# Sliding-window attention with a low-rank mixer: later loads of the low-rank factors, a last tile in halves, and one batch transposed by DMA

## Chip, cores and metric

The kernel runs on one core of a Trainium2 chip. The metric is the device time of one execution in microseconds (us), smaller is better.

## The reference

```python
def _attn_ref(q, k, v):                       # q, k, v: [8, 8, 576, 64]
    scores = (1.0 / np.sqrt(64)) * np.matmul(q, k.transpose(0, 1, 3, 2))
    rel = pos[:, None] - pos[None, :]
    scores = np.where((rel >= 0) & (rel < 64), scores, -1e9)
    attn = softmax(scores)                    # (shortened here)
    return np.matmul(attn, v)

def _moe_ref(x, U, V, w_ch1, w_ch2):          # x: [8, 576, 512], U: [576, 32], V: [32, 576]
    h = x.transpose(0, 2, 1) @ U @ V          # mixes the 576 positions, rank 32
    u = x + h.transpose(0, 2, 1)
    ch = np.maximum(u @ w_ch1, 0.0) @ w_ch2   # MLP, 512 -> 2048 -> 512
    return u + ch
```

The attention output, with the heads side by side, is the `x` of the mixer. Inputs and output are float32. The kernel computes in bf16.

## The kernel before

The output has 8 x 576 = 4608 tokens, and the MLP goes over them in nine chunks of 512. A chunk is a row of "slots": 16 of the first MLP matmul (four TensorE matmuls each, tile `psA`), then 16 quarters of the second (tile `psU`). The attention and the mixer of the next batch are spread over these slots by tables such as `PLACE_2`, so that TensorE does them between MLP matmuls. Batch 0 has no chunk to hide in: everything it needs is the startup, and the first MLP matmul cannot start before it.

The low-rank factors are loaded first of all by SyncE, and the loads that GpSimd issues run beside them:

```python
    load_v(0)                                     # GpSimd; k and q of batch 0 were issued before
    # ... some memsets on VectorE, two of them on uf
    nc.sync.dma_start(
        out=uf[0][:, 0:NFULL, :], in_=moe_U[0 : NFULL * P, :].rearrange("(c p) r -> p c r", p=P)
    )                                             # 512 rows of 128 B
    nc.sync.dma_start(out=uf[0][0:W, NFULL, :], in_=moe_U[NFULL * P : S, :])
    nc.sync.dma_start(out=uf[1][W:P, 0, :], in_=moe_U[0:W, :])
    nc.sync.dma_start(
        out=uf[1][:, 1:NT, :], in_=moe_U[W:S, :].rearrange("(c p) r -> p c r", p=P)
    )
    for g in range(4):
        nc.sync.dma_start(out=vf[g * R : (g + 1) * R, :], in_=moe_V[:, :])   # 32 rows of 2304 B
    w1v = moe_w_ch1.rearrange("(c p) n -> p c n", p=P)
    for lo, hi in ((0, 1024), (1024, 2048)):
        nc.gpsimd.dma_start(out=w1b[:, :, lo:hi], in_=w1v[:, :, lo:hi])      # cast to bf16 on the way
    # ... k, q and v of batch 1, then w2b
```

The startup's main row, and what uses the factors (`K` and `Q` are transposes of k and q by TensorE with the copies behind them, `S` the scores, `PV` the attention output, `U` the product with U, `HT` the product with V):

```python
    for what in ("K0", "K1", "Q0", "Q1", "S0", "S1", "K2", "K3", "Q2", "Q3", "S2", "S3"):
        # ... emits that piece
        turn_over({"K1": 3, "Q1": 1, "S0": 1, "K3": 1, "Q3": 1}.get(what, 0))   # idle matmuls
    # ...
    for i in range(2):
        nc.scalar.copy(out=ub[i][:], in_=uf[i][:])                # ScalarE: U to bf16
    nc.scalar.copy(out=vrep[:, W : W + S], in_=vf[:])             # ScalarE: V to bf16
    for t in range(NT + 2):
        # ... PV(t), XT(t - 2), U(t - 2)
    for f in [a["U"][NT - 1]] + a["X3"] + a["HT"]:
        f()                 # U's last piece copies hh on ScalarE; HT needs hh and vrep
```

From batch 2 on, k and q are transposed by the DMA crossbar, on SyncE's queue; u (the input of the MLP, which must have its features on the partitions) is transposed by TensorE in batches 0 to 2 and by the crossbar from batch 3 on:

```python
    NXU = 3
        def TX(t):                                # k and q of a batch >= 2
            def f():
                for dst, src in ((kx, kb), (qx, qb)):
                    nc.sync.dma_start_transpose(out=dst[:, t, :, :], in_=...)
            return f

        def UT(t):
            def f():
                # ...
                if b >= NXU:
                    nc.sync.dma_start_transpose(out=dst, in_=u_tiles[g][:])
                    return
                tp = ps_tp.tile([P, NDC, P], BF16, name="tpu", tag="tp")
                for dc in range(NDC):
                    nc.tensor.transpose(tp[:, dc, :], u_tiles[g][:, dc * P : (dc + 1) * P], ident[:])
                nc.scalar.copy(out=dst, in_=tp[:])
            return f

    PLACE_2 = {                                   # slots of chunk 1, which carries batch 2
        # ...
        "UTP": [5],                               # batch 1's last transpose
        "TX": [12, 13, 14, 15, 16],               # k and q of batch 3
        "U": [19],
        "V": [21, 22, 23],                        # up-projection: u = V part + x
        "UT": [23, 24, 25, 26, 27],               # u of batch 2
    }
```

SyncE also issues the stores of the outputs (`ch2`, one store of 256 KB per 128 tokens). A store is in program order with the transposes on SyncE.

The softmax here doesn't subtract the row's maximum and nothing guards it: scores larger than these inputs give would overflow.

## Time and profile before

| | us |
|---|---|
| median of the first three runs | 329.75 |
| median of the four runs compared with the kernel after | 330.23 |
| span of the profiled run, granted clock 0.998 | 328.3 |
| first MLP matmul of chunks 0, 1, 2, 3 starts | 24.95, 64.77, 101.54, 135.21 |
| last TensorE instruction starts | 324.19 |

The profile's times count from the start of the span. "L560" is source line 560; the lines of the changed kernel are numbered a little higher, for it is longer. PE is TensorE, DVE VectorE, ACT ScalarE, POOL GpSimd, and SPq is SyncE's sequencer, which issues DMAs. `out<-in` names the tiles.

Here are lines of the page of the kernel before: engine busy time, then the busy tenths in 40 slices of the span (a digit of 9 is 90% or more) for TensorE, its granted clock and the DMA engines, then the chain of waits that ended last.

```profile
span 328.3 us, 6734 instructions
...
PE 316.2 (96%) x2802; PEld 147.9 (45%) x2802; DVE 172.2 (52%) x308; ACT 94.7 (29%) x143; POOL 102.9 (31%) x134
...
PE   6889999989999999999999999999999999999995
...
PEclk9999999999999999999999999999999999999999
DMA  8999999999999999999996993354300330021011
...
## 4 chain that ended last, share of the span: by engine, by line
PE 86%; DVE 5%; ACT 3%; DMA 3%; issue 2%; POOL 1%; POOLq 0%
PE psU L582 38%; PE psA L560 34%; PE xr L364 4%; DMA qg<-in_q_dram 3%; PE sc L311 3%; ACT pts L329 3%; PE psv L486 2%; DVE pts L331 1%; PE pshh L396 1%; DVE un L499 1%; PE tpg L258 1%; PE psht L396 0%; PE psh L396 0%; PE tpu L518 0%; PE ua 
...
```

TensorE is busy for 96% of the span and holds 86% of the chain, at full clock. The DMA engines are nearly full over the first half. What moves the time is therefore when TensorE starts its MLP, and where it waits afterwards.

The startup first. The timeline of ScalarE before shows the casts of U, U and V and the copies of hh (start and duration in us, engine, line, operation; in brackets the idle time before it and what ended it):

```profile
16.97 0.34 ACT L675 CAST ub_97<-uf_95 128x160 bf16<-128x160 f32 x1
17.18 0.35 ACT L675 CAST ub_98<-uf_96 128x160 bf16<-128x160 f32 x1
17.41 0.69 ACT L676 CAST vrep<-vf 128x576 bf16<-128x576 f32 x1
...
23.05 0.65 ACT L406 CAST hh<-psh 128x256 bf16<-128x256 f32 x2 [4.95 <-PE psh L396]
```

And the timeline of TensorE before, first HT matmuls and first MLP matmuls:

```profile
23.47 0.60 PE L464 MATMUL uam<-vrep,hh 128*128 128x512 bf16 x2
...
24.95 1.02 PE L560 MATMUL psA<-uTc,w1b 128*128 128x512 bf16 x4 [0.44 <-DVE uTc L473]
```

The casts are done by 18.1 us, 5 us before ScalarE needs to copy hh. hh ends the startup: the last V load landed at 12.50 us and had slack. The loads of U landed at 2.77, 6.76, 8.22 and 10.76 us.

SyncE next. The timeline of SyncE before: the first issue and the V issues at the start, then the last transpose of batch 3 in chunk 1 and the store behind it. For a transpose the second column is its time on the sequencer.

```profile
0.81 0.45 SPq L199 DMA_DIRECT2D uf_95<-in_moe_U_dram  x1
...
3.97 2.24 SPq L208 DMA_DIRECT2D vf<-in_moe_V_dram  x4
...
92.12 2.54 SPq L280 DMA_TRANSPOSE qf<-qn_111  x1
94.75 8.04 SPq L594 DMA_DIRECT2D out_dram<-osb  x4
```

From 77.43 to 94.66 us SyncE does nothing but batch 3's ten transposes. A store that was ready at 89.5 us leaves at 94.75 and lands at 101.55.

In the waits of TensorE over chunk 1 before (engine, tile, line, waited for: total us, times, longest) there is one only:

```profile
PE tpu L518 <- DVE un L499: 1.1, 1, 1.1
```

### The profile page before, as it was taken

What the parts mean: (1) busy time and instruction counts of PE and PEld (TensorE: products, weight loads), DVE (VectorE), ACT (ScalarE), POOL (GpSimd) and SP (SyncE); (2) the same over time, 40 slices, a digit from 0 to 9 for tenths busy, and PEclk for the clock granted to TensorE, in tenths of its full rate; (3) what the DMA queues carried; (4) which work ended last, traced back from release to release, by engine and by line L of the source; (5) the groups of instructions that cost most, each with busy time, mean ns of one, the idle gap of its engine ahead of it and who ended that gap; (6) DMA issues with size and microseconds to landing.
All of it is one profiled execution on the core that took longest, in us unless ns stands there. A gap on an engine that the chain in (4) does not pass through costs nothing.

```text
span 328.3 us, 6734 instructions
## 1 busy us (share of the span) xinstructions
PE 316.2 (96%) x2802; PEld 147.9 (45%) x2802; DVE 172.2 (52%) x308; ACT 94.7 (29%) x143; POOL 102.9 (31%) x134
## 2 busy tenths in 40 slices
PE   6889999989999999999999999999999999999995
PEld 2444544434454444444444444444444444444442
DVE  4564682378645844584548553765376425115211
ACT  3435641028223530344025401540063001301400
POOL 8591878536536855417700500000000000000000
PEclk9999999999999999999999999999999999999999
DMA  8999999999999999999996993354300330021011
GB/s 114 179 208 195 170 189 169 148 155 175 131 134 208 165 137 154 207 174 141 145 209 98 134 140 112 62 86 103 105 4 2 73 106 32 2 82 45 0 66 64
DMA packets 151871, 39.56 MB, mean 121 GB/s; under 512 B 140960, under 2 KB 146080, under 8 KB 151840
## 3 DMA queue, kind: packets, MB, share of 16 engines
q0 software_dynamic: 100096, 18.36, 78.9%
q1 hardware_dynamic: 51744, 20.77, 35.5%
q8 instruction: 22, 0.36, 0.5%
q14 instruction: 9, 0.07, 0.1%
HBM read 37.14 MB, written 9.44 MB: 142 GB/s over the span
## 4 chain that ended last, share of the span: by engine, by line
PE 86%; DVE 5%; ACT 3%; DMA 3%; issue 2%; POOL 1%; POOLq 0%
PE psU L582 38%; PE psA L560 34%; PE xr L364 4%; DMA qg<-in_q_dram 3%; PE sc L311 3%; ACT pts L329 3%; PE psv L486 2%; DVE pts L331 1%; PE pshh L396 1%; DVE un L499 1%; PE tpg L258 1%; PE psht L396 0%; PE psh L396 0%; PE tpu L518 0%; PE ua L447 0%
## 5 line engine op out<-in xcount | busy, mean ns | idle before, releaser
L560 PE MATMUL psA<-uTc,w1b 128*128 128x512 bf16 x576 | 133.7, 380 | 2.3 <-DVE uTc L473 0.4
L560 PEld LDWEIGHTS <-w1b 128*128 128x128 bf16 x576 | 53.3, 98 | 63.3 <-issue 2.9
L591 DVE TENSOR_TENSOR osb<-psU,un 128x512 f32<-128x512 f32 x36 | 24.8, 689 | 78.0 <-PE psU L582 78.0
L329 ACT ACTIVATE pts<-sc 128x1024 bf16<-128x1024 f32 x32 | 31.3, 1023 | 8.8 <-PE sc L311 7.3
L331 DVE TENSOR_TENSOR pts<-pts,maskA 128x1024 bf16<-128x1024 bf16 x28 | 19.3, 691 | 10.2 <-ACT pts L329 10.2
L135 POOL DMA_DIRECT2D vA_105<-in_v_dram x16 | 14.1, 885 | 29.4 <-DVE c_9_2735 L569 18.3
L499 DVE TENSOR_TENSOR un<-psv,xs_102 128x512 bf16<-128x512 f32 (+1 forms) x20 | 13.0, 683 | 10.4 <-PE psv L486 10.4
L135 POOL DMA_DIRECT2D vA_104<-in_v_dram x16 | 14.1, 887 | 13.4 <-PE xr L364 7.9
L499 DVE TENSOR_TENSOR un<-psv,xs_103 128x512 bf16<-128x512 f32 (+1 forms) x20 | 13.0, 684 | 8.6 <-PE psv L486 8.4
L364 PEld LDWEIGHTS <-pts 128*64 128x64 bf16 x512 | 11.2, 110 | 10.4 <-issue 4.1
L126 POOL DMA_DIRECT2D kn_108<-in_k_dram x15 | 12.7, 847 | 10.1 <-DMA vA_105<-in_v_dram 5.8
L126 POOL DMA_DIRECT2D qn_110<-in_q_dram x15 | 12.7, 848 | 8.7 <-DMA qn_110<-in_q_dram 4.5
L126 POOL DMA_DIRECT2D kn_109<-in_k_dram x15 | 12.8, 857 | 6.4 <-DMA vA_104<-in_v_dram 3.9
L373 DVE RECIPROCAL rcp<-xr 128x8 f32<-128x8 f32 (+1 forms) x40 | 8.2, 204 | 12.8 <-PE xr L364 12.4
L311 PEld LDWEIGHTS <-kf 64*64 64x64 bf16 x704 | 10.1, 107 | 10.2 <-issue 9.1
L374 DVE TENSOR_TENSOR xs_103<-xr,rcp 128x512 bf16<-128x512 f32 (+1 forms) x20 | 13.8, 692 | 0.7
L374 DVE TENSOR_TENSOR xs_102<-xr,rcp 128x512 bf16<-128x512 f32 (+1 forms) x20 | 13.8, 690 | 0.7
L126 POOL DMA_DIRECT2D qn_111<-in_q_dram x15 | 12.8, 855 | 2.8 <-DMA qn_111<-in_q_dram 2.1
L486 PE MATMUL psv<-hh,vrep 128*128 128x512 bf16 x40 | 12.6, 379 | 0.0
L311 PE MATMUL sc<-qf,kf 64*64 64x128 bf16 (+1 forms) x576 | 11.2, 214 | 0.0
L635 PE MATMUL unread<-idle 128*128 128x512 bf16 x16 | 6.4, 524 | 1.3 <-DVE idle L156 1.3
L364 PE MATMUL xr<-vA_105,pts 128*64 128x65 bf16 x160 | 7.2, 197 | 0.2 <-DVE xs_103 L374 0.2
(553 smaller groups left out, 510.0 us busy)
## 6 DMA issues: line engine op xcount, KB each, us to landing
out_dram<-osb SPq DMA_DIRECT2D x36, 256.0 KB, 3.0
vA_104<-in_v_dram POOLq DMA_DIRECT2D x16, 128.0 KB, 8.1
w1b<-in_moe_w_ch_dram POOLq DMA_DIRECT2D x2, 1024.0 KB, 15.0
vA_105<-in_v_dram POOLq DMA_DIRECT2D x16, 128.0 KB, 11.5
w2b<-in_moe_w_ch_dram POOLq DMA_DIRECT2D x4, 512.0 KB, 12.6
kn_108<-in_k_dram POOLq DMA_DIRECT2D x12, 128.0 KB, 11.9
qn_110<-in_q_dram POOLq DMA_DIRECT2D x12, 128.0 KB, 13.2
kn_109<-in_k_dram POOLq DMA_DIRECT2D x12, 128.0 KB, 10.8
```

Source lines behind the costliest of these rows:

```text
L126: nc.gpsimd.dma_start(out=dst[0:rows, t, :, :], in_=src[b, :, t * P : t * P + rows, :].rearrange("h p d -> p h d"),)
L135: nc.gpsimd.dma_start(out=va[:, t, :, 0:D], in_=v[b, :, t * P : (t + 1) * P, :].rearrange("h p d -> p h d"),)
L311: nc.tensor.matmul(sc[r0 : r0 + W, g, col * W : (col + n) * W], keys_of(j, u, rs), queries_of(j, blk, n, rs), start=not spare, stop=last o ...
L329: nc.scalar.activation(out=dst, in_=sc[:], func=ACT.Exp, scale=scale)
L331: nc.vector.tensor_tensor(out=dst, in0=dst, in1=maskA.rearrange("p g n w -> p g (n w)"), op=ALU.mult)
L364: nc.tensor.matmul(xr[r0 : r0 + W, h // 4, (h % 4) * VW : (h % 4 + 1) * VW], pts[:, h // 2, h % 2, blk, :] if blk < NB - 1 else ptl[:, h / ...
L374: nc.vector.tensor_tensor(out=x[lo:hi, t, :, :].rearrange("p (a h) d -> p a h d", a=2), in0=xv[:, :, :, 0:D], in1=rcp[lo:hi].to_broadcast( ...
L486: nc.tensor.matmul(ps[0][:, n, :], vrep[:, off : off + P], hh["sb"][:], start=True, stop=True)
L499: nc.vector.tensor_tensor(out=u_tiles[g][rs, :], in0=ps[0][rs, n, :], in1=x[rs, t, :, :].rearrange("p h d -> p (h d)"), op=ALU.add,)
L560: nc.tensor.matmul(ps[:], w1b[:, dc, i * P : (i + 1) * P], uTc[:, :, dc, :], start=(dc == 0), stop=(dc == NDC - 1),)
L582: nc.tensor.matmul(acc[t][:], c1[i][:, t * P : (t + 1) * P], w2b[:, i, :], start=(i == 0), stop=(i == NFC - 1),)
L591: nc.vector.tensor_tensor(out=osb[:], in0=acc[t][:], in1=u_tiles[g][:], op=ALU.add)
```

## The change

It has three parts. (1) The loads of U and V leave only after the copy of K3 (small memsets on VectorE into their tiles make SyncE wait for VectorE), so that q, k and v of batch 0 get the DMA engines first. (2) The last output tile of 128 tokens is computed in two halves of 256 columns, and each half is stored by two queues, to shorten the end. (3) u of batch 2 is transposed by the crossbar in place of TensorE, its up-projection comes one slot sooner, the transposes follow in slots 20 to 22, and batch 1's last transpose moves from slot 5 to 7.

```diff
-    NXU = 3
+    NXU = 2
...
-    nc.vector.memset(uf[0][:, NT - 1, :], 0.0)
-    nc.vector.memset(uf[1][:, 0, :], 0.0)
...
-    (the eight nc.sync.dma_start of U and V, as above)
+    def load_low_rank():
+        for part in (uf[0][:, NT - 1, :], uf[0][:, 0, 0:1], uf[1][:, 0, :], uf[1][:, 1, 0:1], vf[:, 0:1]):
+            nc.vector.memset(part, 0.0)
+        (the same eight nc.sync.dma_start)
...
+        def ch2_last(t, quarter):
+            def f():
+                ...
+                half = quarter // 2
+                cs = slice(half * DM // 2, (half + 1) * DM // 2)
+                ...                       # 8 matmuls per quarter, 256 columns each
+                if quarter % 2 == 1:
+                    osb = out_pool.tile([P, DM], FP32, name="osb")[:, 0 : DM // 2]
+                    nc.vector.tensor_tensor(out=osb, in0=acc[half][:], in1=u_tiles[g][:, cs], op=ALU.add)
+                    for r0, queue in ((0, nc.sync), (W, nc.scalar)):
+                        queue.dma_start(
+                            out=outf[g * P + r0 : g * P + r0 + W, cs], in_=osb[r0 : r0 + W, :]
+                        )
+            return f
+
         def ch2(t, quarter):
+            if c == NCH - 1 and t == TPC - 1:
+                return ch2_last(t, quarter)
...
     PLACE_2 = {
-        "UTP": [5],
+        "UTP": [7],
...
-        "V": [21, 22, 23],
-        "UT": [23, 24, 25, 26, 27],
+        "V": [20, 21, 22],
+        "UT": [20, 21, 21, 22, 22],
     }
...
             a["T"][2 * j + (what[0] == "Q")]()
+        if what == "K3":
+            load_low_rank()
```

More of the change, by code (lines that the diff above doesn't have):

```diff
@@ L196 @@
         nc.vector.memset(qn[i][W:P, NFULL, :, :], 0.0)
-    nc.sync.dma_start(
-        out=uf[0][:, 0:NFULL, :], in_=moe_U[0 : NFULL * P, :].rearrange("(c p) r -> p c r", p=P)
-    )
-    nc.sync.dma_start(out=uf[0][0:W, NFULL, :], in_=moe_U[NFULL * P : S, :])
-    nc.sync.dma_start(out=uf[1][W:P, 0, :], in_=moe_U[0:W, :])
-    nc.sync.dma_start(
-        out=uf[1][:, 1:NT, :], in_=moe_U[W:S, :].rearrange("(c p) r -> p c r", p=P)
-    )
-    for g in range(4):
-        nc.sync.dma_start(out=vf[g * R : (g + 1) * R, :], in_=moe_V[:, :])
+    def load_low_rank():
+        for part in (uf[0][:, NT - 1, :], uf[0][:, 0, 0:1], uf[1][:, 0, :], uf[1][:, 1, 0:1], vf[:, 0:1]):
+            nc.vector.memset(part, 0.0)
+        nc.sync.dma_start(
+            out=uf[0][:, 0:NFULL, :], in_=moe_U[0 : NFULL * P, :].rearrange("(c p) r -> p c r", p=P)
+        )
+        nc.sync.dma_start(out=uf[0][0:W, NFULL, :], in_=moe_U[NFULL * P : S, :])
+        nc.sync.dma_start(out=uf[1][W:P, 0, :], in_=moe_U[0:W, :])
+        nc.sync.dma_start(
+            out=uf[1][:, 1:NT, :], in_=moe_U[W:S, :].rearrange("(c p) r -> p c r", p=P)
+        )
+        for g in range(4):
+            nc.sync.dma_start(out=vf[g * R : (g + 1) * R, :], in_=moe_V[:, :])
     w1v = moe_w_ch1.rearrange("(c p) n -> p c n", p=P)
@@ L574, in mlp @@
         acc = {}
+        def ch2_last(t, quarter):
+            def f():
+                g = c * TPC + t
+                half = quarter // 2
+                cs = slice(half * DM // 2, (half + 1) * DM // 2)
+                if quarter % 2 == 0:
+                    acc[half] = psum["mm"].tile([P, DM // 2], FP32, name="psL", tag="mm")
+                for i in range(8 * (quarter % 2), 8 * (quarter % 2) + 8):
+                    nc.tensor.matmul(
+                        acc[half][:],
+                        c1[i][:, t * P : (t + 1) * P],
+                        w2b[:, i, cs],
+                        start=(i == 0),
+                        stop=(i == NFC - 1),
+                    )
+                if quarter % 2 == 1:
+                    osb = out_pool.tile([P, DM], FP32, name="osb")[:, 0 : DM // 2]
+                    nc.vector.tensor_tensor(
+                        out=osb, in0=acc[half][:], in1=u_tiles[g][:, cs], op=ALU.add
+                    )
+                    for r0, queue in ((0, nc.sync), (W, nc.scalar)):
+                        queue.dma_start(
+                            out=outf[g * P + r0 : g * P + r0 + W, cs], in_=osb[r0 : r0 + W, :]
+                        )
+            return f
         def ch2(t, quarter):
+            if c == NCH - 1 and t == TPC - 1:
+                return ch2_last(t, quarter)
             def f():
```

## The prediction

> **What bounds the kernel now.** TensorE: busy 316 of 328.3 us in the engine summary, 86% of the chain of waits, granted clock 0.998. It idles only at the start (first MLP matmul at 24.95 us), about 1 us per chunk, and at the end (last matmul issued 324.19, end 328.3). The DMA engines are nearly full until about 170 us (slices view). In the packet records two DMA queues that both have work alternate packet for packet: 40 stores of 2048 B beside 40 loads of 128 B per quarter microsecond at 101 us, 62 beside 62 at 8.3 us. (The Trainium skill, DMA: Bandwidth & Descriptors, section Queues, rings and completion order, has this round robin; this trace agrees.)
>
> **Part 1, low-rank loads held back.** They leave SyncE after the K3 copy on VectorE, which ends at 12.8 us. Gain: the last q load landed at 12.77 us while 1,280 low-rank packets alternated with it. It would land 1 to 1.5 us sooner, but VectorE's copies and added memsets (0.3 us) leave only 0.3 us. Cost: the v loads (128 B packets, 1,100 per us) are through by about 14 us then, and the weight load w1b follows at 103 packets of 2048 B per us. The two U copies need 1,152 packets, so alternation makes this about 10 us (estimate: packets over rate), then V. V lands near 26 to 30 us instead of 12.5. ScalarE casts U, U, V in order before it copies hh (23.05 before), so TensorE's HT matmuls (23.47) start 4 to 8 us late. I take +6.
>
> **Part 2, last tile in halves.** The last VectorE add goes from 0.69 to about 0.37 us and the last store (2.0 us to landing) shrinks: -0.6. Same matmul time.
>
> **Part 3, u of batch 2 by crossbar.** Removed: 16 TensorE transposes. The matmul groups there are 1.08 us apart instead of 0.86: -0.9. Moving batch 1's transpose from slot 5 to 7 avoids a 1.1 us wait for VectorE, but slot 6 waits anyway for q transposes that land at 73.7, so little. Cost: SyncE issues in order, and its timeline shows it occupied by batch 3's ten k and q transposes from 77.4 to 94.7 us; a store ready at 89.5 leaves only at 94.75 and lands at 101.55. The new transposes come after that store; each is 512 packets, 1.3 to 1.6 us, so the third (the last that chunk 2 needs) lands near 105.8 on the old clock, where TensorE now arrives at 100.8. Stall 3 to 5 us, taken +4. The earlier up-projection doesn't help, for SyncE is the limit.
>
> Also: two TensorE pauses near 4 us may lower its clock (Trainium skill, TensorE: Matmul & The Clock Gate, part 1; not shown here): +1. The DMA backlog shrinks while TensorE waits: -1.5.
>
> **Sum.** 329.75 - 0.3 + 6 - 0.6 - 0.9 + 4 + 1 - 1.5 = 337.5 us. Range 328.5 to 343. Chances: faster by over 2% 0.02, within 2% 0.40, slower 0.58.
>
> **What would show it.** Right: V cast and hh near 28 us with TensorE idle before HT; first MLP matmul near 30; TensorE waiting for a uTc transpose ahead of chunk 2; uTc transposes issued just after the last q transpose. Wrong: V landed before 22 us, or no gap at chunk 2.
>
> **What would make it wrong.** U packets slip in while v packets are still queued (v is fast, so 1 us of shift saves many); then part 1 gains a little. Or batch 3's transposes run faster once other loads have drained; then part 3 gains its 0.9. With both, about 327.5.

## More of the kernel before

The granted TensorE clock of each trace is given where it matters. Executions of one kernel on one chip spread over about 1% here, so small differences are judged from several rounds.

Last, the busy time by stretches of the startup, before; the columns are as its first line names them, and PEclk is the granted clock:

```profile
core 0: us, PE busy (x) PEld busy (x) DVE busy (x) ACT busy (x) POOL busy (x), PEclk, DMA share, GB/s
17.00:25.00 8.00, 6.84 (x93) 3.33 (x89) 5.33 (x12) 2.82 (x8) 7.37 (x10) 1.00 1.12 210
25.00:35.00 10.00, 10.00 (x57) 4.50 (x59) 4.48 (x8) 4.78 (x8) 2.71 (x4) 1.00 1.87 185
```

TensorE is busy and its clock is 1.00 in both stretches.

## The result

| | before | after |
|---|---|---|
| median of 4 runs | 330.23 us | 345.01 us |
| lowest to highest | 329.72 to 331.37 | 342.87 to 346.18 |
| span of the profiled run, granted clock | 328.3, 0.998 | 341.2, 0.975 |

The ratio of after to before is 1.0435, with a 95% interval of 1.0373 to 1.0498: slower. Here and below a ratio is the mean time of one kernel's fast runs over the mean of the other's in the same rounds, so it is not quite the ratio of the medians quoted. The profiled run of the kernel after is the fastest of its four (342.87 us), so the trace shows less than the usual loss: its span is 12.8 us longer.

The starts of the first MLP matmul of each chunk, read from the timelines of TensorE, tell where the 12.8 us are. A chunk's length is the difference of two starts.

| us | before | after | difference |
|---|---|---|---|
| start of chunk 0 | 24.95 | 34.64 | +9.69 |
| length of chunk 0 | 39.81 | 41.60 | +1.79 |
| length of chunk 1 | 36.78 | 38.23 | +1.45 |
| length of chunk 2 | 33.67 | 33.48 | -0.19 |
| length of the last chunk | 27.41 | 27.56 | +0.15 |
| from the last TensorE start to the end | 4.13 | 4.09 | -0.04 |

The chunks between are alike within 0.01 us. Three quarters of the loss is the startup. It is well outside the scatter of single traces: in the five traces whose startup is that of the kernel before (before, e5 to e8 below) chunk 0 starts between 24.70 and 28.11 us.

The same lines of the page, for the kernel after:

```profile
span 341.2 us, 6728 instructions
...
PE 317.5 (93%) x2779; PEld 150.0 (44%) x2802; DVE 171.9 (50%) x312; ACT 92.6 (27%) x139; POOL 102.8 (30%) x134
...
PE   6755999998999799999999999999999999999995
...
PEclk9957799999999999999999999999999999999999
DMA  7999999999999979998999698153410170011012
...
## 4 chain that ended last, share of the span: by engine, by line
PE 73%; DMA 13%; DVE 5%; SPq 3%; ACT 3%; issue 2%; POOL 1%; POOLq 0%; ACTq 0%
PE psA L563 32%; PE psU L614 29%; DMA vf<-in_moe_V_dram 4%; DMA uTc<-un 4%; PE xr L367 3%; DMA qf<-qn_110 3%; PE sc L314 2%; DMA qg<-in_q_dram 2%; PE psv L489 2%; ACT pts L332 2%; SPq L283 1%; DVE pts L334 1%; PE psL L587 1%; PE pshh L399 1
...
```

The clock row now has a 5 and two 7s in the slices from 17 to 43 us, and the chain of waits has 13% of DMA where it had 3%. The loads of V (`vf`) and the transposes of u (`uTc<-un`) are named in it.

ScalarE's timeline after, the same casts and copies:

```profile
24.01 0.33 ACT L709 CAST ub_97<-uf_95 128x160 bf16<-128x160 f32 x1 [7.86 <-DMA uf_95<-in_moe_U_dram]
...
28.58 0.33 ACT L709 CAST ub_98<-uf_96 128x160 bf16<-128x160 f32 x1 [4.24 <-DMA uf_96<-in_moe_U_dram]
...
31.73 0.67 ACT L710 CAST vrep<-vf 128x576 bf16<-128x576 f32 x1 [2.82 <-DMA vf<-in_moe_V_dram]
32.31 0.64 ACT L409 CAST hh<-psh 128x256 bf16<-128x256 f32 x2
```

TensorE's timeline after:

```profile
33.13 0.63 PE L467 MATMUL uam<-vrep,hh 128*128 128x512 bf16 x1 [4.10 <-ACT hh L409]
...
34.64 1.87 PE L563 MATMUL psA<-uTc,w1b 128*128 128x512 bf16 x4
```

Every cast now waits for its load: 7.86 and 4.24 us for the two of U, 2.82 us for V. The last V load landed at 31.63 us, 19.1 us later than before. hh then waits behind V's cast on ScalarE, and HT starts at 33.13 in place of 23.47.

SyncE's timeline after: first issue and V issues, then in chunk 1 the last transpose of batch 3, the store behind it, and the new transposes:

```profile
12.28 0.46 SPq L201 DMA_DIRECT2D uf_95<-in_moe_U_dram  x1
...
15.74 2.29 SPq L210 DMA_DIRECT2D vf<-in_moe_V_dram  x4
...
101.29 1.73 SPq L283 DMA_TRANSPOSE qf<-qn_111  x1
103.11 1.06 SPq L626 DMA_DIRECT2D out_dram<-osb  x1
104.27 6.15 SPq L517 DMA_TRANSPOSE uTc<-un  x4
```

The low-rank loads are issued 11.5 us later, yet they land up to 20 us later: from issue to landing they take 11 to 14 us. The new transposes of u stand behind the batch's k and q transposes and a store, as predicted; they landed at 111.74, 112.88, 114.33 and 115.87 us. TensorE's waits over chunk 1, after:

```profile
PE psA L563 <- DMA uTc<-un: 2.3, 1, 2.3
PE sc L314 <- DMA qf<-qn_110: 1.1, 1, 1.1
```

So 2.3 us for u (third transpose, just ahead of chunk 2), and 1.1 us for a q transpose. And the stretches of the startup, after (columns as for before):

```profile
17.00:25.00 8.00, 3.77 (x44) 1.80 (x46) 2.70 (x6) 0.33 (x1) 6.85 (x9) 0.55 1.24 216
25.00:35.00 10.00, 5.88 (x45) 2.68 (x47) 2.82 (x6) 2.72 (x6) 1.50 (x2) 0.67 2.05 194
```

TensorE is busy for 3.77 of 8 us in the first of them, and the granted clock is 0.55 and 0.67.

A count of the packet records from the trace of the kernel after tells what the low-rank loads met. It is a tabulation of mine, not a view of the profile: packets that started in each microsecond.

```
 us    queue 0 (GpSimd's)                queue 1 (SyncE's)
 16     91, mostly 2048 B (w1b)           20, 128 B (U)
 17    100, 2048 B                        81, 128 B
 18    102, 2048 B                       103, 128 B
 19    107, 2048 B                       107, 128 B
 20    104, 2048 B                       103, 128 B
 25    190, mostly 768 B                 189, mostly 128 B
 28    212, mostly 768 B                  36, mostly 2304 B (V)
 30    281, mostly 768 B                   5, mostly 2304 B
```

Each queue gets as many packets as the other, whatever their size. The 1,152 packets of U can then go no faster than the 2048 B packets of the weight beside them. This agrees with the Trainium skill, "DMA: Bandwidth & Descriptors", section "Queues, rings and completion order", which says that each DMA engine round-robins between the queue rows that it has work for, packet by packet. The first U packet starts at 16.36 us, 4.1 us after its issue; before, on DMA engines that were still empty, it was 1.1 us.

### The profile page after: what moved, and what is told of

It is laid out like the page before. It is cut to its first block, busy times and chain, and to the rows that moved or that the text cites. A ratio compares the mean times of both kernels' runs of the same rounds, so it can differ in the third digit from the quotient of the medians.

```text
span 341.2 us, 6728 instructions
## 1 busy us (share of the span) xinstructions
PE 317.5 (93%) x2779; PEld 150.0 (44%) x2802; DVE 171.9 (50%) x312; ACT 92.6 (27%) x139; POOL 102.8 (30%) x134
## 4 chain that ended last, share of the span: by engine, by line
PE 73%; DMA 13%; DVE 5%; SPq 3%; ACT 3%; issue 2%; POOL 1%; POOLq 0%; ACTq 0%
PE psA L563 32%; PE psU L614 29%; DMA vf<-in_moe_V_dram 4%; DMA uTc<-un 4%; PE xr L367 3%; DMA qf<-qn_110 3%; PE sc L314 2%; DMA qg<-in_q_dram 2%; PE psv L489 2%; ACT pts L332 2%; SPq L283 1%; DVE pts L334 1%; PE psL L587 1%; PE pshh L399 1%; PE tpg L261 1%
## 5 line engine op out<-in xcount | busy, mean ns | idle before, releaser
L332 ACT ACTIVATE pts<-sc 128x1024 bf16<-128x1024 f32 x32 | 31.4, 1024 | 10.8 <-PE sc L314 10.4
L314 PEld LDWEIGHTS <-kf 64*64 64x64 bf16 x704 | 10.2, 107 | 11.4 <-issue 11.2
L126 POOL DMA_DIRECT2D qn_110<-in_q_dram x15 | 13.2, 881 | 5.4 <-DMA qf<-qn_110 2.9
L126 POOL DMA_DIRECT2D qn_111<-in_q_dram x15 | 13.0, 866 | 1.3 <-DMA qf<-qn_111 0.6
L367 PE MATMUL xr<-vA_104,pts 128*64 128x65 bf16 x160 | 6.8, 204 | 1.3 <-issue 1.0
L367 PE MATMUL xr<-vA_105,pts 128*64 128x65 bf16 x160 | 7.2, 197 | 0.2 <-DVE xs_103 L377 0.2
## 6 DMA issues: line engine op xcount, KB each, us to landing
w2b<-in_moe_w_ch_dram POOLq DMA_DIRECT2D x4, 512.0 KB, 12.8
```

The source lines that it names most:

```text
L126: nc.gpsimd.dma_start(out=dst[0:rows, t, :, :], in_=src[b, :, t * P : t * P + rows, :].rearrange("h p d -> p h d"),)
L314: nc.tensor.matmul(sc[r0 : r0 + W, g, col * W : (col + n) * W], keys_of(j, u, rs), queries_of(j, blk, n, rs), start=not spare, stop=last o ...
L332: nc.scalar.activation(out=dst, in_=sc[:], func=ACT.Exp, scale=scale)
L367: nc.tensor.matmul(xr[r0 : r0 + W, h // 4, (h % 4) * VW : (h % 4 + 1) * VW], pts[:, h // 2, h % 2, blk, :] if blk < NB - 1 else ptl[:, h / ...
```

## The experiments

My theory had three statements. At the start, U and V share turns with w1b's large packets, and the number of packets sets how long they take. In chunk 1, SyncE issues in order, so u of batch 2 queues behind batch 3's transposes. TensorE's waits lower its clock, and that is charged on top. The rivals: at the start, that the loads are late only because they are issued late, at whatever company; that it is the lowered clock that costs most and not the wait; in chunk 1, that the new slots of the up-projection cost or gain something of themselves.

### Part 1 alone (e1_held)

The changed kernel with parts 2 and 3 undone:

```diff
-    NXU = 2                   (PLACE_2 as before)
+    NXU = 3
-            if c == NCH - 1 and t == TPC - 1:
-                return ch2_last(t, quarter)
```

> Part 1 alone (low-rank loads held back until after the K3 copy; the last tile and batch 2 as before). If the late start of the MLP is part 1's doing, nearly all of the loss is here: first MLP matmul near 34.6 us as in the changed kernel (24.95 before), V landed at 30 to 32 us, and the whole 10 to 12.5 us over before. Rival: the transposes of batch 2 are the larger cost; then this run is under 6 us over before.

Measured: correct, 339.67 us (338.08 to 340.36) beside 330.73, ratio 1.0267 (1.0220 to 1.0314). V landed at 31.36 us, HT started at 32.46, and the first MLP matmul at 34.37, against 24.95 before. Chunk 0 took 40.27 us (39.81 before), and the later chunks as before. The medians are 8.9 us apart, a little less than the 10 to 12.5 expected, but far from the rival's "under 6". Part 1 gives the startup's whole delay by itself.

### Fewer packets for U (e2_rows512)

Part 1 alone, with the two large copies of U as 128 rows of 512 B in place of 512 rows of 128 B: the same bytes in a quarter of the packets. The rows go to wrong places, so the result is wrong (relative error 0.78).

```diff
-            out=uf[0][:, 0:NFULL, :], in_=moe_U[0 : NFULL * P, :].rearrange("(c p) r -> p c r", p=P)
+            out=uf[0][:, 0:NFULL, :], in_=moe_U[0 : NFULL * P, :].rearrange("(p c) r -> p c r", p=P)
-            out=uf[1][:, 1:NT, :], in_=moe_U[W:S, :].rearrange("(c p) r -> p c r", p=P)
+            out=uf[1][:, 1:NT, :], in_=moe_U[W:S, :].rearrange("(p c) r -> p c r", p=P)
```

> Part 1 alone with the two large U copies read as 128 rows of 512 B each instead of 512 rows of 128 B: the same bytes, 768 packets fewer (wrong result on purpose: rows of U land on other partitions). If the queues alternate packet for packet with the 2048 B packets of w1b, U and V land about 768/103 = 7 us sooner, V near 24 us, first MLP matmul near 26 to 27 us, and the total is within 3 us of before. Rival (bytes, or the late issue and the latency of a busy queue set the arrival): V lands near 31 us as in the changed kernel and the total stays 10 us or more over before.

Measured: 335.46 us (333.85 to 336.11) beside 330.73, ratio 1.0139 (1.0093 to 1.0186). U's last copy landed at 23.15 us, 5.7 us sooner than in part 1 alone, and V at 27.07, 4.3 us sooner; both loads were issued no sooner. TensorE's timeline of this run, the first HT matmuls:

```profile
28.16 0.95 PE L467 MATMUL uam<-vrep,hh 128*128 128x512 bf16 x2 [3.16 <-ACT hh L409]
```

The first MLP matmul was at 29.99 us, 4.4 us sooner. So the number of packets does cost the time, and the rival of the late issue alone falls. But I had expected V near 24 us and a total within 3 us of before, and it stayed 4.7 us above: the first packet again started only at 16.75 us, 3.9 us after its issue, and V was last again. The packets were not all of it.

### No company for U and V (e3_gate)

Part 1 alone, with w1b and every later load issued by GpSimd only after V has landed:

```diff
-    w1v = ...                                  (w1b, then k, q, v of batch 1, and w2b, issued here)
+    gate = const.tile([P, 1], FP32, name="gate")
+    def load_rest():
+        nc.gpsimd.tensor_copy(out=gate[:], in_=vf[:, 0:1])
+        (the same loads)
...
             load_low_rank()
+            load_rest()
```

> Part 1 alone, and w1b (with all the loads after it) issued only when V has landed, so that the low-rank packets have nothing of 2048 B to alternate with. If the alternation is the cause, V lands at 18 to 20.5 us (SyncE issues its last copy near 17.6, 2 us to land); w1b then starts near 20 and its first half lands near 26 to 27, which sets the first MLP matmul at 27 to 28 us; total 3 to 6 us over before. Rival (late issue, queue latency): V lands after 27 us and the total is worse than part 1 alone.

Measured: correct, 337.58 us (336.47 to 337.83) beside 330.73, ratio 1.0204 (1.0162 to 1.0246). U landed at 17.03 to 17.51 us, V at 18.40 to 19.23, 12 us sooner than in part 1 alone, although they were issued at the same times within a microsecond. From 16 to 17 us, 570 packets of SyncE's queue started beside 7 of the other, where the kernel after had 101 to 107 of each per us from 18 to 24 us. The first packet started 1.3 us after its issue, while v's packets (844 in that microsecond) were still running. TensorE's timeline:

```profile
22.44 0.60 PE L472 MATMUL uam<-vrep,hh 128*128 128x512 bf16 x2
...
27.78 1.70 PE L568 MATMUL psA<-uTc,w1b 128*128 128x512 bf16 x4 [4.31 <-DMA w1b<-in_moe_w_ch_dram]
```

HT started a microsecond sooner than before the change. The wait has then moved to w1b, which landed at 27.74 us. The total is a little over the 3 to 6 us expected, because the later loads came late too: chunk 0 took 42.55 us, 2.7 us more than before, with a stretch at half clock from 28.0 to 31.4 us. This is the clearest of the experiments, though it takes away the late first packet and the sharing of turns together: the same loads take 2 to 5 us from issue to landing alone, and 11 to 14 us beside w1b.

### Keeping TensorE busy while it waits (e4_warm and e9_warm2)

Part 1 alone, with idle matmuls (on a tile of zeros, into an open accumulation, so the result is unchanged) at the two places where TensorE waits for U and V. The first version had 20 and 19 turns of them, the second 15 and 11:

```diff
             a["XT"][t - 2]()
+            if t == 2:
+                a["idle"](20)              # e9_warm2: 15
             a["U"][t - 2]()
...
-    for f in [a["U"][NT - 1]] + a["X3"] + a["HT"]:
+    for f in [a["U"][NT - 1]] + a["X3"]:
+        f()
+    a["idle"](19)                          # e9_warm2: 11
+    for f in a["HT"]:
         f()
```

> Part 1 alone with matmuls on zeros put before the two waits (80 of 128 columns before U is used, 76 before HT; the result is unchanged). The waits stay, V lands at the same time. If the lowered clock after the waits is worth about 2 us (the first MLP chunk was 1.8 us longer in the changed kernel), the granted clock is 1.0 from 17 us on and the total is 1.5 to 3 us below part 1 alone. Rival (clock does not matter, TensorE waits for ScalarE and DMA anyway): the same total within 0.7 us.

e4_warm: correct, 339.00 us (338.28 to 339.34) beside 330.73, ratio 1.0247 (1.0198 to 1.0295). That is 0.7 us below part 1 alone in the same rounds, the rival's figure, and the clock was not full throughout as expected: it was half from 18.4 to 21.8 us. But the test is spoilt: V landed at 30.44 us, the idle matmuls ran on, and HT started only at 33.12 (33.28 in the next expectation). Chunk 0 took 39.81 us, exactly as before.

> Part 1 alone with fewer matmuls on zeros in the two waits (60 and 44 of 128 columns, 3.4 and 2.5 us at full clock), so that they end before U and V are there, as those of the earlier run did not (its HT started at 33.28 us though V had landed at 30.44). If the lowered clock is a real cost of these waits, the first chunk takes 39.8 us instead of 40.3 to 41.6, HT to the first MLP matmul takes 1.5 us instead of 2.0, and the total is 1 to 2 us below part 1 alone (ratio to before 1.020 to 1.024 against 1.0267). Rival: no difference over 0.5 us.

e9_warm2: correct, 338.76 us (338.04 to 340.31) beside 331.51, ratio 1.0210 (1.0170 to 1.0251); part 1 alone had 1.0267 on another chip. The first MLP matmul was at 33.32 us, chunk 0 took 39.81. The stretches, with columns as above:

```profile
17.00:25.00 8.00, 5.53 (x102) 4.42 (x99) 2.67 (x6) 0.32 (x1) 6.66 (x9) 1.00 1.25 216
25.00:35.00 10.00, 9.53 (x98) 5.90 (x99) 3.26 (x7) 3.18 (x7) 1.50 (x2) 0.83 2.00 196
```

The clock still fell once, from 25.2 to 28.6 us, but was full for HT and the MLP. The ratio lies in the expected range, but its interval overlaps with that of part 1 alone, so the totals do not show a gain. The traces show where one would be: from HT to the first MLP matmul 1.48 us in place of 1.91, and chunk 0 0.45 us shorter than in e1_held, together 0.9 us for the clock; the rest of this trace's lead is V, which happened to land 1.0 us sooner (30.34). With the clock full for HT and the MLP the start is still 8.4 us later than before: the wait is by far the larger cost, so the rival that puts the loss on the clock falls.

### Part 2 alone (e5_halves)

The kernel before with `ch2_last` added, as in the diff above.

> Part 2 alone (last tile in halves). The changed kernel's end (last matmul issued to the end of the span) was 4.09 us against 4.13, and its last chunk 0.15 us longer: a total within 0.3 us of before, no gain. My prediction had -0.6 us; that would show as an end of 3.5 us.

Measured: correct, 332.30 us (331.02 to 334.15) beside 331.63, ratio 1.0015 (0.9980 to 1.0049). There is no gain. The trace of the kernel after shows why, and that of this run agrees within 0.02 us: the last add takes 0.42 us in place of 0.69, but of the two stores behind it ScalarE's landed 2.22 us after its issue (SyncE's 1.96), where one store took 2.01 us. Counted from the start of the last matmul, the last store lands 0.15 us sooner (2.99 against 3.14), and that matmul itself starts 0.15 us later in its chunk. The Trainium skill, "DMA: Bandwidth & Descriptors", section "Rules for kernel authors", says of two transfers to disjoint partition halves: "Don't bother". This agrees as far as it goes: the halves, 64 KB each, landed no sooner than one store of 256 KB did. No run stored the half tile by one queue.

### Part 3 alone (e6_crossbar), its places alone (e7_places), and another order (e8_order)

e6_crossbar is the kernel before with `NXU = 2` and the new places; e7_places has the new places with `NXU = 3`.

> Part 3 alone (batch 2's u by crossbar, new places). If the transposes wait behind batch 3's k and q transposes on SyncE, chunk 2's first matmul waits 2.5 to 5 us for the third of them, which is issued at 97 to 99 us and lands at 104 to 106; 0.9 us of transposes on TensorE is saved; total 1.5 to 4 us over before. Rival (the wait in the changed kernel came from the shifted start, which put other loads beside these transposes): no wait over 0.6 us at chunk 2 and a total 0.5 to 1.2 us below before.

e6_crossbar: correct, 338.21 us (336.93 to 339.98) beside 331.63, ratio 1.0194 (1.0161 to 1.0227). The last transpose of batch 3 was issued at 92.11 us, a store at 94.90, the transposes of u at 95.54, 97.04, 98.41 and 99.96, and they landed at 103.19, 104.55, 106.01 and 107.62. TensorE's waits over chunk 1, and the stretch after the wait (columns as above):

```profile
PE psA L560 <- DMA uTc<-un: 5.5, 1, 5.5
PE sc L311 <- DMA qf<-qn: 1.1, 1, 1.1
```

```profile
104.00:111.00 7.00, 4.85 (x45) 2.06 (x46) 0.69 (x1) 1.25 (x2) 3.34 (x5) 0.51 1.74 219
```

The third landed at 106.01 us, the first matmul of chunk 2 started at 106.15, and TensorE had waited 5.5 us. The clock was half from 104.2 to 111.0 us, and chunk 2 took 35.73 us in place of 33.67. I had expected 1.5 to 4 us in total and measured 6.6: the clock was missing from that sum.

> Only the new places of part 3, the transposes still on TensorE (batch 1's last transpose in slot 7 instead of 5, up-projection of batch 2 one slot sooner, its transposes in slots 20 to 22). Slot 6 waits for the q transposes that land near 73.7 us either way, so the total is within 0.5 us of before; a transpose that follows its addition at once may make TensorE wait for VectorE by up to 1 us more in slots 20 to 22. Rival: the removed wait of 1.1 us before the transpose in slot 5 is a gain of about 1 us.

e7_places: correct, 332.14 us (330.93 to 333.53) beside 331.63, ratio 1.0009 (0.9980 to 1.0038). Its profiled chunk 1 took 38.70 us, 1.9 more than in the trace before, but over five rounds the kernels are the same, so I draw nothing from that one trace. The places alone neither cost nor gain more than about 1 us (the interval is -0.2% to +0.4%), and that rival falls.

e8_order is e6_crossbar with the last two of batch 3's transposes behind those of u:

```diff
-        "TX": [12, 13, 14, 15, 16],
+        "TX": [12, 13, 14, 23, 24],
```

> Part 3 alone, with the last four k and q transposes of batch 3 moved behind the u transposes on SyncE (slots 23 and 24 instead of 15 and 16). If SyncE's order is what makes the u transposes late, the third of them is issued about 3 to 4 us sooner (near 94 to 95 us) and lands near 101.5 to 103, so that chunk 2's first matmul waits 0.5 to 2.5 us instead of 2.5 to 5; the moved transposes then land near 108 us or later and the scores of batch 3 in slot 1 of chunk 2 wait for them, 3 us or more: the total is no better. If not SyncE's order but the landing under load is what counts, the wait at chunk 2 stays.

e8_order: correct, 337.14 us (335.03 to 338.50) beside 331.63, ratio 1.0155 (1.0115 to 1.0196). Its waits:

```profile
PE sc L311 <- DMA qf<-qn: 3.6, 2, 3.1
PE psA L560 <- DMA uTc<-un: 0.9, 1, 0.9
```

The wait for u falls from 5.5 to 0.9 us, so it was SyncE's order that made it. (The startup of the profiled run was itself 3.2 us late, but that did not speed up the queue: counted from the start of chunk 1, the sixth of batch 3's transposes was issued at 20.24 us, in e6_crossbar at 20.47, while the third transpose of u was issued at 28.83 in place of 33.69.) But 3.1 us of a new wait are there, for the q transpose that was moved back, and chunk 2 is 38.24 us long. The total is hardly better than e6_crossbar's: in neither of the two orders did SyncE's queue take four more transposes in this window without a wait.

### The loads by another queue (e10_sw and e11_sw2)

If two busy queues take turns, U and V can share the queue that carries everything else, at their place in its order. e10_sw is the kernel before with U and V loaded by GpSimd, cast to bf16 on the way, which also takes away three casts on ScalarE; GpSimd's copies for v of batch 0 move to VectorE.

```diff
-    (eight nc.sync.dma_start of U and V into uf, vf; w1b in two halves by nc.gpsimd)
+    nc.gpsimd.dma_start(out=ub[0][:, 0:NFULL, :], in_=u4)
+    nc.gpsimd.dma_start(out=ub[0][0:W, NFULL, :], in_=moe_U[NFULL * P : S, :])
+    nc.gpsimd.dma_start(out=w1b[:, :, 0:1024], in_=w1v[:, :, 0:1024])
+    for g in range(4):
+        nc.gpsimd.dma_start(out=vrep[g * R : (g + 1) * R, W : W + S], in_=moe_V[:, :])
+    nc.gpsimd.dma_start(out=w1b[:, :, 1024:2048], in_=w1v[:, :, 1024:2048])
+    (the two copies of U into ub[1], by nc.gpsimd)
...
-    (three nc.scalar.copy: uf to ub, uf to ub, vf to vrep)
```

> A version meant to keep the gain of part 1 without its cost: before, with U and V loaded by GpSimd's own queue, behind batch 0's q, k and v and around the first half of w1b, cast to bf16 on the way, so that nothing alternates with them (ScalarE's three casts and the fp32 staging go; the shift copies of v of batch 0 move to VectorE). If alternation is what cost part 1, V lands at 20 to 22 us, batch 0's last q load still lands about 1 us sooner than in before, and the first MLP matmul starts at 23.8 to 24.6 us (24.95 before): total 0.3 to 1.2 us below before. Rival (any later load of U and V delays the MLP): 25.5 us or later and a total above before.

Measured: correct, 330.65 us (329.94 to 331.17) beside 331.51, ratio 0.9956 (0.9922 to 0.9990). The last q load landed at 11.33 us in place of 12.77, so the intent of part 1 is reached without its price. V landed at 23.08 us, and TensorE's timeline shows HT waiting for it:

```profile
23.22 0.59 PE L459 MATMUL uam<-vrep,hh 128*128 128x512 bf16 x2 [0.67 <-DMA vrep<-in_moe_V_dram]
...
24.68 1.02 PE L555 MATMUL psA<-uTc,w1b 128*128 128x512 bf16 x4 [0.44 <-DVE uTc L468]
```

e11_sw2 cuts w1b's first half in two and puts V between the cuts:

```diff
-    nc.gpsimd.dma_start(out=w1b[:, :, 0:1024], in_=w1v[:, :, 0:1024])
+    nc.gpsimd.dma_start(out=w1b[:, :, 0:512], in_=w1v[:, :, 0:512])
     (the four loads of V)
+    nc.gpsimd.dma_start(out=w1b[:, :, 512:1024], in_=w1v[:, :, 512:1024])
```

> The software-queue version of e10_sw with one thing moved: the first half of the first MLP weight is cut in two, and the four copies of V are issued between the two cuts, so that V no longer queues behind all of that half. If V is what still limits the start in e10_sw (last V landed 23.08 us, HT at 23.22), V should land between 18.5 and 20.5 us, HT start near 22.7 us and the first MLP matmul near 24.1 us (24.95 before, 24.68 in e10_sw); total 0.3 to 1 us below e10_sw, ratio to before 0.992 to 0.996. Rival: the chain of q, PV and un of batch 0 or the first half of w1b limits already, then V lands sooner but the first MLP matmul stays within 0.2 us of 24.7 and the ratio within 0.001 of 0.9956.

Measured: correct, 332.29 us (331.22 to 334.21) beside 332.33, ratio 1.0018 (0.9979 to 1.0056). V landed at 20.50 us, at the late edge of what was expected, and no TensorE wait for it was left. But the first MLP matmul was at 25.76 us, and both theories missed. The stretches show why:

```profile
14.00:18.00 4.00, 2.31 (x64) 1.53 (x66) 2.67 (x10) 2.13 (x3) 1.85 (x4) 0.99 1.75 155
18.00:21.00 3.00, 3.00 (x43) 1.40 (x39) 2.11 (x5) 0.00 (x0) 3.00 (x5) 0.50 0.85 108
```

The clock was half from about 18 to 21 us, although there was no wait longer than 1.0 us ahead of it: TensorE was busy for 2.31 of the 4 us from 14 to 18. e10_sw was busy for 2.45 of the same 4 us and kept its clock at 1.00. It is not the new order that makes this. The trace of e5_halves, whose startup is that of the kernel before, has such a stretch too (18.7 to 22.2 us), and its first MLP matmul is at 26.57. So the clock of this stretch hangs on little, whatever the version, and one trace of each can't rank them. Of the two versions one has a ratio just under 1 and the other just over it, so I claim no improvement.

## Why the prediction was wrong

The direction and the two mechanisms were right, but the time was predicted as 337.5 us, with up to 343, and was 345.0. In the order of its sum, with the traced run of the kernel after (span +12.84 us; the sum was +7.7):

| term of the sum | predicted | in the trace of after |
|---|---|---|
| earlier q loads and later V together, at the first MLP matmul | -0.3 + 6 | +9.69 |
| lowered clock | +1 | +1.79, chunk 0 |
| transposes taken from TensorE | -0.9 | -0.85 |
| stall ahead of chunk 2, less the shrunken backlog | +4 - 1.5 | +2.29 |
| last tile in halves (length of the last chunk, and the end) | -0.6 | +0.15 - 0.04 |

The remaining -0.19 us is chunk 2. The transposes' -0.85 was not timed by itself: it is what the waits leave of chunk 1, as said below. Of the 5.1 us by which the traced run exceeds the sum, 4.0 are in the first row.

- **The step that failed is the size of part 1, "I take +6".** The prediction had V landing "near 26 to 30 us" and HT "4 to 8 us late". V landed at 31.63 us and HT was 9.66 us late. The turn-taking was right, down to the 103 packets per us. What I mis-sized is when it begins and how it ends. I counted from about 14 us, when v would be through; v's last packets started in the microsecond from 15, and the first U packet only at 16.36 us. I rounded down, too: 1,152 packets at 103 per us are 11.2 us, not 10. And at the end SyncE's queue started its last 52 packets, 31 of them rows of V, only from 28 to 31 us, while the other queue started over 200 per us. e1_held shows that part 1 alone makes this delay, e2_rows512 that the packets count for 4 to 6 us of it, e3_gate that the company is all of it. In e3_gate U's packets did slip in among v's, which the prediction named as what would save part 1; with w1b queued behind v they did not.
- **The gain of part 1 was real and worth nothing.** q landed 0.9 us sooner (11.83 us), more than the 0.3 that I gave it, but HT waits for V anyway.
- **The clock was right in kind and too small.** It was said to be not shown by the trace before. The trace after shows half clock from 17.8 to 28.0 and from 31.5 to 38.3 us. The MLP began at 34.64 us, so 3.64 us of it at half clock, worth at most half of that, are in chunk 0, and this is the +1.79. In the first stretch TensorE had nothing to do for much of the time; for part 1 alone the traces of e9_warm2 and e1_held put the cost at 0.9 us. The Trainium skill, "TensorE: Matmul & The Clock Gate", Part 1, has the clock halved after an idle window of about 3.4 us; the half-clock stretches of these traces come in steps of 3.41 us, which agrees with the length of that window; that it need not be idle throughout, see the last section.
- **The stall of part 3 was right, and so was what weakens it.** By itself the third transpose landed at 106.01 us, where 105.8 was predicted, and the stall was 5.5 us. In the kernel after it is 2.3 us, because batch 3's ten transposes are done 26.8 us after chunk 1's start and not 29.9: 103.02 less 76.24, against 94.66 less 64.77. With the startup so late, the DMA engines had more of their backlog behind them. This is the prediction's "DMA backlog shrinks", and the two terms together, +2.5, are what was measured. The runs of part 1 alone bear this out: with the MLP's start at 33.3 to 34.6 us (e1_held, e4_warm, e9_warm2) the ten are done 27.3 to 27.6 us after chunk 1's start, and in e3_gate, where the other loads were held back as well, 30.6.
- **The transposes were right.** Chunk 1 is 1.45 us longer. Its new waits are 2.3 us for u and 1.1 for q, its old wait of 1.1 us is gone, and this leaves -0.85 for the 16 transposes taken out, a remainder. The same sum for e6_crossbar, with 5.5 for 2.3, gives 4.65, which is what its chunk 1 measured.
- **The tail gained nothing.** The shorter add is eaten by ScalarE's slower store and by the last chunk, 0.15 us longer where the prediction had "Same matmul time".
- **The parts add up, roughly.** Ratios of 2.67%, 0.15% and 1.94% alone make 4.8%, and together they are 4.35%. By the traces the difference should be larger: in company the stall is 3.2 us smaller and chunk 2 keeps its clock (2.1 us), against 1.3 us more in chunk 0. The parts were measured on different chips, so this is a rough check.

Three things stay open. The three runs that were not traced are up to 3.3 us longer than the traced one, with mean granted clocks of 0.968 to 0.975 (its own is 0.975), and I cannot say where. Why SyncE's queue runs thin at its end, 36 to 5 packets per us, cannot be read from counts by queue. And no run shows why its first packet came about 4 us after the issue when w1b was queued behind v, and 1.3 us after it when w1b was not.

## What to carry to other kernels

A load that is held back does not only start later: it starts in the company of whatever is queued by then, and if it is made of many small packets beside large ones, it can take as long as the same number of large ones, as U did here. Before you delay a transfer, count its packets and look at what the other queue holds at the new time; before you add work to an engine that issues in order, add up what stands ahead of it at that slot, and add the lowered clock to the wait. And look at what a saving frees: a sooner q was worth nothing here, for it was not what the next step waited for.

## What the Trainium skill lacked or had wrong

- "DMA: Bandwidth & Descriptors", section "Queues, rings and completion order", gives the round robin in packets but does not spell out the consequence for time: beside 2048 B packets, queue 1 started 101 to 107 packets, most of 128 B, per us, beside almost nothing 570. While both queues were full, a load's time in company was its packets over the other queue's packet rate.
- The same page, "Latency and other measured facts", gives a first byte of about 600 ns for DMAs from SyncE. Here the first packet started 1.1 us after the start of the issue on empty DMA engines, 0.65 us after its end, which is near that figure. It was 1.3 us after the start beside v's loads alone (e3_gate), and 3.9 to 4.1 us with w1b queued behind v (e2_rows512, after). For busy engines the page gives an access latency of the memory but no first byte.
- "TensorE: Matmul & The Clock Gate", Part 1, speaks of an idle window of about 3.4 us. In e11_sw2 the clock was halved after a stretch with no wait over 1.0 us, in which TensorE was busy for 2.31 of 4 us; in e10_sw 2.45 of 4 us left it full. The page tells of a kernel whose many short pauses made the clock swing, but gives no threshold. The 13 traces narrow it down (a tabulation from their clock records, not a view): within each trace every change of the clock falls on a step of 3.41 us. Up to chunk 2, TensorE was busy for at most 1.85 us of the step ahead of a fall (e5_halves) and for at least 1.96 us of a step that kept the full clock (e2_rows512). At the end of the kernel four steps with 1.44 to 1.82 us kept it, so busy time alone is not the measure.
- No page that I used says how thin a queue may run at its end: the last 52 packets of SyncE's queue, 31 of them rows of V, were spread over three microseconds (36, 11 and 5) while the other queue started more than 200 per us.
